# A fused retention and gated MLP kernel: another start, pair 3 transposed by DMA, and loads in turns behind a gate

## The chip, the cores and the metric

The kernel runs on one core of a Trainium2 chip. The metric is the device time in microseconds (us) of a whole execution, the median of several runs. A profile shows one execution: its span runs from the first to the last instruction of the core, and the execution's own time is somewhat longer.

## The reference

Linear attention with a decay per head (a retention layer), and behind it an MLP whose activation is h·cos(h):

```python
gamma = 1.0 - 2.0 ** (-5.0 - np.arange(H))
for t in range(S):
    state = gamma * state + einsum('bhd,bhe->bhde', k[:, :, t], v[:, :, t])
    y[:, :, t] = scale * einsum('bhd,bhde->bhe', q[:, :, t], state)
x = y.transpose(0, 2, 1, 3).reshape(B * S, H * D)
h = x @ w_in
out = (h * np.cos(h)) @ w_out
```

There are B = 4 batches, H = 8 heads, S = 768 positions and D = 64; x has 3072 rows of 512, w_in is 512 x 2048, w_out 2048 x 512. All inputs and the output are float32; inside, the products run in bf16.

## The kernel before

**Tiling.** A sequence is cut into 6 chunks of 128 positions. The unit of the attention is a *pair*: one chunk of two batches, so there are 12 pairs, numbered 0 to 11. Two pairs make a *group* of 512 rows for the MLP; there are 6 groups. A pair's q, k and v are float32 buffers of 128 positions x 8 heads x 64, one per batch (the two *halves* of a pair, 256 KB each). There are five sets of them, and `SLOT` says which set a pair uses.

**What a pair goes through.** `load` fetches q, k and v. `conv_q` multiplies q by its decay and `conv_v` does so with v, mostly on GpSimd; `conv_k` casts k to bf16 on ScalarE. Then q and k are transposed: either by `stage_t` (16 transposes on TensorE and two VectorE copies out of PSUM) or by `stage_t_dma` (two DMA transposes issued by SP, one for each half). `stage_a` (A) multiplies k by q, `stage_m` (M) applies the causal mask on VectorE, `half_y` (Y) forms the outputs of a half, with the carried state if the chunk isn't the first, and ScalarE copies them to `xt`, the MLP's input. `stage_s` (S) adds the chunk to the state in PSUM, and `state_out` copies that to `stb` for the next pair.

**What a group goes through.** `unit_f` is one of 16 units of the first MLP matmul: four matmuls over 512 rows, a sine on ScalarE (cos(h) = sin(h + pi/2)), and a product on VectorE into `gt`. `pair_f` is the same for the 256 rows of one pair, two units at a time, and `first_f` the first four units of group 0. `unit_o` is a quarter of a 128-row output tile: four matmuls; behind the fourth quarter ScalarE copies the tile to one of four buffers `ob`, and SP issues its copy to memory. In the main loop the units F of group g and O of group g-1 alternate, in 16 slots s per group.

**What sets the order.** The schedule is manual: each engine runs its instructions in the order in which the program text issues them, and waits by semaphores for data and for buffers. `Clock` and `Banks` are bookkeeping while the program is built: they choose which of the seven PSUM banks a unit takes, by an estimate of when each comes free. A bank is free once its reader on ScalarE or VectorE is done, so work that stands late in ScalarE's order holds TensorE's banks.

**The queues.** Loads are issued by GpSimd for the most part (L132, and L138 for k of pair 1, both halves in one transfer). SP issues the first q, the first k and the second q (L163), and q and a part of v of pairs 4 and 5 (L495 and L498). The DMA transposes (L240) and the output copies (L387) are SP's. GpSimd's loads of a pair stand behind the products of an earlier pair in its order. No load waits for a transpose unless a buffer makes it.

**Start.** Pairs 0 and 1 run ahead of everything, with dummy matmuls (`warm`) between their stages. In L465 to L475 the order is A(1, half 0), Y(0, half 0), A(1, half 1), S(0), Y(0, half 1), three dummies, Y(1, half 0), Y(1, half 1), S(1), and then `first_f` (L476).

**Later pairs.** Pairs 2 and 3 are transposed on TensorE (L485 and L505), pairs 4 to 11 by DMA. From pair 6 on the main loop decides by the slot (L588 to L603): at slots 0 and 8 `ahead(p + 1)` issues the products and casts of the next pair, a slot later its transposes, and further slots A, M, Y and, inside `later`, the next loads. The k casts of pairs 7, 8, 9, 10 and 11 so stand behind F units (2,0), (2,8), (3,0), (3,8) and (4,0), where (g, s) is slot s of group g.

Of the kernel before, what the change touches and what calls it, by code (L numbers as in the profile page):

```python
# [47 lines left out]
def kernel(  # L48
# [50 lines left out]

    qf = [[sb([128, H, D], FP32, f"qf{i}_{b}") for b in range(2)] for i in range(PRE)]  # L100
    kf2 = [sb([128, 2, H, D], FP32, f"kf{i}") for i in range(PRE)]
    kf = [[t[:, b] for b in range(2)] for t in kf2]
    vf = [[sb([128, H, D], FP32, f"vf{i}_{b}") for b in range(2)] for i in range(PRE)]
    ob = [sb([128, DM], FP32, f"ob{i}") for i in range(4)]
# [14 lines left out]
    gk = sb([128, NC, H], FP32, "gk")  # L119
    rel = sb([128, 128], FP32, "rel")  # L120


# [12 lines left out]

    def load_k(p):
        bp, c = divmod(p, NC)
        nc.gpsimd.dma_start(  # L138
            out=kf2[SLOT[p]].rearrange("p b h d -> p (b h) d"),
            in_=k[2 * bp : 2 * bp + 2, :, ds(c * C, C)].rearrange("b h t d -> t (b h) d"))  # L140

# [16 lines left out]
    def w_in_t(i, f):  # L158
# [3 lines left out]

    load(nc.sync, 0, ("q0", "k0", "q1"))  # L163
    nc.gpsimd.iota(pos, pattern=[[C, NC]], base=1, channel_multiplier=1,
                   allow_small_or_imprecise_dtypes=True)
    nc.gpsimd.iota(rel, pattern=[[1, 128]], base=0, channel_multiplier=-1,
                   allow_small_or_imprecise_dtypes=True)
    load(nc.gpsimd, 0, ("k1",))
    load(nc.gpsimd, 1, ("q0", "q1"))
    load_k(1)  # L170
    load(nc.gpsimd, 0, ("v0", "v1"))
# [292 lines left out]
    clk.run("pe", 0.0, 11.8)  # L464
    stage_m(1, stage_a(1, 0))  # L465
    half_y(0, 0)
    clk.run("pe", 0.0, 12.4)
    stage_m(1, stage_a(1, 1))
    stage_s(0, nc.scalar.copy)
    half_y(0, 1)  # L470
    warm(3)
    half_y(1, 0)
    banks.give(spare, clk.pe)
    half_y(1, 1)
# [7 lines left out]
    for u in range(12):  # L482
        unit_o(0, u % 4, u // 4)
        if u == 7:
            stage_t(2, 0)  # L485
            stage_t(2, 1)
            conv_v(2, nc.vector, (0,))
        elif u == 9:
            stage_m(2, stage_a(2, 0))
            conv_v(2, nc.vector, (1,))  # L490
        elif u == 11:
            stage_m(2, stage_a(2, 1))
    conv_k(3, True)
    conv_q(3, nc.gpsimd)
    load(nc.sync, 4, ("q0", "q1"))  # L495
    load(nc.gpsimd, 4, ("k0", "k1", "v0", "v1"))
    conv_v(3, nc.gpsimd)
    load(nc.sync, 5, ("q0", "q1", "v0"))  # L498
    load(nc.gpsimd, 5, ("k0", "k1", "v1"))
    for j in range(4):  # L500
# [3 lines left out]
    pair_f(2, 0)  # L504
    stage_t(3, 0)  # L505
    stage_t(3, 1)
    pair_f(2, 1)
    attend(3)
    conv_q(4, nc.gpsimd)
    conv_v(4, nc.gpsimd)  # L510
    conv_k(4, True)
    stage_t_dma(4)
    load(nc.gpsimd, 6, ("q0", "k0", "q1", "k1", "v0", "v1"))
    pair_f(2, 2)
    pair_f(2, 3, (0,))
    stage_y(3, nc.scalar.copy)
    pair_f(2, 3, (1,))
    conv_q(5, nc.gpsimd)
    conv_v(5, nc.gpsimd)
    load(nc.gpsimd, 7, ("q0", "k0", "q1", "k1", "v0", "v1"))  # L520
    pair_f(3, 0)
    conv_k(5, True)
    stage_t_dma(5)
    pair_f(3, 1)
    pair_f(3, 2)
    conv_q(6, nc.gpsimd)
    conv_k(6, True)
    conv_v(6, nc.gpsimd)
    pair_f(3, 3)

    def ahead(p):
        if p < NP:
            conv_q(p, nc.gpsimd)
            conv_k(p, True)
            conv_v(p, nc.gpsimd)

    def fetch(p):
        load(nc.gpsimd, p, ("q0", "k0", "q1", "k1", "v0", "v1"))

    def later(p):  # L540
        stage_y(p)
        n = 8 if p == 4 else p + 3 if p > 5 else NP
        if n < NP:
            fetch(n)

# [19 lines left out]
    attend(4)  # L565
    stage_t_dma(6)
    o_units(1, 2, 6)
    later(4)
    attend(5)
    o_units(1, 6, 10)  # L570
    later(5)

    for g in range(2, NG + 1):
        for s in range(16):
            hf, r = divmod(s, 8)
            p = 2 * (g + 1) + hf
# [9 lines left out]
            while late and late[0][0] <= 16 * g + s:  # L586
                late.pop(0)[1]()
            if p < NP:  # L588
                if r == 0:
                    ahead(p + 1)  # L590
                elif r == 1:
                    if p + 1 < NP:
                        stage_t_dma(p + 1)
                elif r == 2 and p in (6, 7, 8):
                    todo = [stage_a(p, b) for b in range(2)]
                    stage_m(p, todo[0])
                    put_off(16 * g + s + 1, lambda todo=todo, p=p: stage_m(p, todo[1]))
                elif r == 6 and p in (6, 7, 11):
                    later(p)
                elif (g, s) == (3, 4):  # L600
                    fetch(11)
                if (g, s) in joined:
                    join(joined[g, s], 16 * g + s)  # L603

# [29 lines left out]
```

## Time and profile before

| | us |
|---|---|
| median of 8 runs | 209.2 |
| lowest, highest | 209.01, 209.64 |
| the profiled execution's own time | 209.49 |
| its span | 207.7 |

| engine | busy us | share of the span |
|---|---|---|
| TensorE matmul (PE) | 200.2 | 96% |
| TensorE weight load (PEld) | 113.0 | 54% |
| VectorE (DVE) | 113.2 | 55% |
| ScalarE (ACT) | 114.4 | 55% |
| GpSimd (POOL) | 102.4 | 49% |

A busy time is the sum of an engine's instructions. GpSimd's includes the issuing of its loads here, though not that of other engines' DMAs, and its work ends at about 123 us of the span. TensorE is busy in nearly all of the span, and its granted clock is full throughout. The 16 DMA engines are close to fully busy from the start up to about 115 us and have little to do after that. In all, 27.26 MB are read from memory and 6.29 MB written. The chain of waits is followed back from the last instruction, at each step to what released it; a list of waits says which engine stood still, for whom, for how long in total, how often, and for how long at most. In a timeline a row has the start, the duration, the engine and line, the operation, and in brackets the idle time before it and what ended that.

### The profile page before, as it was taken

The numbers are of one execution on the slowest core, as the hardware profiler recorded it, in microseconds if no ns is written. First come the engines' busy times: TensorE is split into PE (matmuls) and PEld (weight loads), VectorE is DVE, ScalarE is ACT, GpSimd is POOL, SyncE is SP. The second block draws the span as 40 slices with busy tenths as digits, with TensorE's granted clock in tenths as the row PEclk, the third lists the DMA queues.
The fourth block names the chain that finished last, engine by engine and source line by source line (L and its number), as shares of the span: only waits on it lengthen the run. The fifth ranks groups of instructions, "written<-read, shape, count | busy, mean of one in ns | idle before, by whom it ended". The sixth has DMA issues, their size and how long they took to land.

```text
span 207.7 us, 4176 instructions
## 1 busy us (share of the span) xinstructions
PE 200.2 (96%) x1646; PEld 113.0 (54%) x1646; DVE 113.2 (54%) x188; ACT 114.4 (55%) x193; POOL 102.4 (49%) x118
## 2 busy tenths in 40 slices
PE   7689999999999999999999999999999999999993
PEld 2257554559897555546544465544465444444452
DVE  4691984554956563869874367853367244443000
ACT  6678873247997336577753754653554653553120
POOL 8999238399999999999996130000000000000000
PEclk9999999999999999999999999999999999999999
DMA  6999999999999999949999711161101101110212
GB/s 159 345 237 206 214 253 286 336 270 347 236 152 298 337 204 299 288 155 194 196 292 139 205 43 50 54 104 50 50 3 50 50 15 39 50 52 20 81 75 80
DMA packets 36644, 33.83 MB, mean 163 GB/s; under 512 B 26768, under 2 KB 29072, under 8 KB 36624
## 3 DMA queue, kind: packets, MB, share of 16 engines
q0 software_dynamic: 7808, 20.98, 39.1%
q1 hardware_dynamic: 28672, 12.49, 27.1%
q8 instruction: 13, 0.21, 0.4%
q10 hardware_dynamic: 144, 0.10, 0.1%
q14 instruction: 7, 0.06, 0.1%
HBM read 27.26 MB, written 6.29 MB: 162 GB/s over the span
## 4 chain that ended last, share of the span: by engine, by line
PE 92%; DMA 3%; DVE 2%; issue 1%; SPq 0%; ACT 0%; DVEq 0%
PE bank L379 39%; PE bank L338 32%; PE bank L349 7%; PE bank L257 3%; DMA qf<-in_q_dram 3%; PE bank L279 3%; PE bank L284 3%; PE bank L396 2%; PE st_ps L301 1%; DVE am L266 1%; PE bank L360 1%; PE bank L230 1%; PE bank L367 1%; DVE qkt L214 1%; SPq L132 0%
## 5 line engine op out<-in xcount | busy, mean ns | idle before, releaser
L331 DVE TENSOR_TENSOR gt<-bank,cosb 128x512 bf16<-128x512 f32 x96 | 64.9, 689 | 62.7 <-ACT cosb L327 62.5
L327 ACT ACTIVATE cosb<-bank,halfpi 128x512 bf16<-128x512 f32 x96 | 65.1, 688 | 49.9 <-PE bank L338 45.4
L379 PE MATMUL bank<-w_out_sb,gt 128*128 128x512 bf16 x368 | 89.6, 379 | 0.0
L338 PE MATMUL bank<-xt,w_in 128*128 128x512 bf16 x304 | 75.3, 380 | 0.0
L379 PEld LDWEIGHTS <-gt 128*128 128x128 bf16 x368 | 35.5, 98 | 41.3
L338 PEld LDWEIGHTS <-w_in 128*128 128x128 bf16 x304 | 33.9, 114 | 30.7
L266 DVE TENSOR_TENSOR am<-bank,mask 128x512 bf16<-128x512 f32 x48 | 30.4, 682 | 3.8 <-PE bank L257 3.7
L202 POOL TENSOR_TENSOR vs<-vf,gk 128x512 bf16<-128x512 f32 x21 | 21.4, 1044 | 6.0 <-PE st_ps L301 5.9
L386 ACT COPY ob<-bank 128x512 f32<-128x512 f32 x23 | 13.4, 587 | 17.9 <-PE bank L379 17.9
L132 POOL DMA_DIRECT2D vf<-in_v_dram x23 | 20.3, 885 | 4.6 <-DMA w_out_sb<-in_moe_w_out_dram 4.6
L195 POOL TENSOR_TENSOR qk<-qf,gq 128x512 bf16<-128x512 f32 x18 | 18.6, 1055 | 5.0 <-DMA qf<-in_q_dram 2.8
L132 POOL DMA_DIRECT2D kf<-in_k_dram x21 | 18.9, 901 | 1.8 <-DMA w_out_sb<-in_moe_w_out_dram 1.6
L208 ACT CAST qk<-kf 128x512 bf16<-128x512 f32 x24 | 14.0, 615 | 9.5 <-DMA kf<-in_k_dram 9.5
L288 ACT CAST xt<-bank 128x512 bf16<-128x512 f32 x24 | 13.0, 588 | 7.9 <-PE bank L284 7.8
L132 POOL DMA_DIRECT2D qf<-in_q_dram x18 | 16.2, 902 | 0.8 <-DMA w_in<-in_moe_w_in_dram 0.8
L349 PE MATMUL bank<-xt,w_in 128*128 128x256 bf16 x128 | 14.7, 273 | 0.0
L349 PEld LDWEIGHTS <-w_in 128*128 128x128 bf16 x128 | 13.8, 114 | 0.4
L284 PE MATMUL bank<-am,vs 128*64 128x128 bf16 x192 | 11.7, 220 | 0.0
L279 PEld LDWEIGHTS <-stb 128*64 128x64 bf16 x160 | 8.8, 109 | 4.3 <-issue 3.1
L279 PE MATMUL bank<-qkt,stb 128*64 128x128 bf16 x160 | 10.7, 222 | 0.1
L284 PEld LDWEIGHTS <-vs 128*64 128x64 bf16 x192 | 10.0, 110 | 0.5 <-issue 0.4
L313 DVE CAST stb<-st_ps 64x512 bf16<-64x512 f32 x12 | 8.2, 685 | 2.3 <-PE st_ps L301 2.1
(46 smaller groups left out, 85.5 us busy)
## 6 DMA issues: line engine op xcount, KB each, us to landing
vf<-in_v_dram POOLq DMA_DIRECT2D x23, 256.0 KB, 6.9
out_dram<-ob SPq DMA_DIRECT2D x23, 256.0 KB, 2.0
kf<-in_k_dram POOLq DMA_DIRECT2D x21, 256.0 KB, 6.7
qf<-in_q_dram POOLq DMA_DIRECT2D x18, 256.0 KB, 6.2
w_out_sb<-in_moe_w_out_dram POOLq DMA_DIRECT2D x4, 512.0 KB, 12.3
qf<-in_q_dram SPq DMA_DIRECT2D x6, 256.0 KB, 8.2
w_in<-in_moe_w_in_dram POOLq DMA_DIRECT2D x3, 512.0 KB, 8.1
kf<-in_k_dram POOLq DMA_DIRECT2D x1, 512.0 KB, 6.0
```

The source lines that it names most:

```text
L132: eng.dma_start(out=t[SLOT[p]][b], in_=src[2 * bp + b, :, ds(c * C, C)].rearrange("h t d -> t h d"))
L195: eng.tensor_tensor(out=qk[p % NB][:, b, 0], in0=qf[SLOT[p]][b], in1=bc(gq, p % NC), op=ALU.mult)
L202: eng.tensor_tensor(out=vs[p % NB][:, b], in0=vf[SLOT[p]][b], in1=bc(gk, p % NC), op=ALU.mult)
L208: nc.scalar.copy(out=qk[p % NB][:, b, 1], in_=kf[SLOT[p]][b])
L266: nc.vector.tensor_tensor(out=am[p % 2][b][j], in0=ap[j], in1=mask.unsqueeze(1).to_broadcast([128, HP, 128]), op=ALU.mult)
L279: nc.tensor.matmul(yp[ts(j, 64), a, :], lhsT=stb[p % 2][:, b, a, ts(j, 64)], rhs=qt(n, b, a), start=True, stop=False, skip_group_check=True)
L284: nc.tensor.matmul(yp[ts(j, 64), a, :], lhsT=vs[n][:, b, 2 * a + j, :], rhs=am[p % 2][b][j][:, a, :], start=(c == 0), stop=True, skip_grou ...
L327: nc.scalar.activation(out=cb, in_=bank, func=AF.Sin, bias=halfpi)
L331: nc.vector.tensor_tensor(out=out, in0=bank, in1=cb, op=ALU.mult)
L338: nc.tensor.matmul(bank, lhsT=w_in_t(i, f), rhs=xt[g % 2][:, i, :], start=(i == 0), stop=(i == KIN - 1))
L349: nc.tensor.matmul(bank[:, ts(e, 256)], lhsT=w_in_t(i, f + e), rhs=xt[g % 2][:, i, ts(hf, 256)], start=(i == 0 and e == 0), stop=(i == KIN ...
L379: nc.tensor.matmul(bank, lhsT=gt[g % 2][:, f, ts(j, 128)], rhs=w_out_sb[:, f, :], start=(f == 0), stop=(f == KOUT - 1))
```

## The change

- **First loads.** k of pair 0, half 0, is issued by ScalarE (its own hardware queue), q of pair 0, half 0, by SP, and after it q of pair 1, half 0. The second q of pair 0 is issued by GpSimd, behind the second k.
- **Order of the start.** S(0) comes directly behind A(1, half 0), then A(1, half 1), and then both halves of Y(0). The three dummies are split: one ahead of Y(1, half 0), two behind it.
- **Pair 3** is transposed by DMA, no longer on TensorE. Its k casts are issued at u = 9 of the loop over the first output units, no longer behind that loop.
- **Turns.** From pair 3 on, `turn(p)` issues on GpSimd the q products, has SP issue the DMA transposes, issues the v products, and then a copy of two columns out of the transposed k of half 0 into a scratch tile `gate`, which nobody reads. The loads of pair p+1 follow it, as three transfers of 512 KB (k, q, v, both halves in each). GpSimd works in order, so these loads aren't issued until the transposition of half 0 is complete. SP issues no loads any more after the start. The q, k and v buffers of a pair's two halves are now one tile.
- **Places.** The k casts get places of their own: pair 4 behind `pair_f(2, 0)`, pair 5 where it was, pair 6 within the first output units of group 1, and pairs 7 to 11 behind (2,0), (2,6), (2,12), (3,4) and (3,12). A and Y keep their places on TensorE.

```diff
-    qf = [[sb([128, H, D], FP32, f"qf{i}_{b}") for b in range(2)] for i in range(PRE)]
-    kf2 = [sb([128, 2, H, D], FP32, f"kf{i}") for i in range(PRE)]
-    kf = [[t[:, b] for b in range(2)] for t in kf2]
-    vf = [[sb([128, H, D], FP32, f"vf{i}_{b}") for b in range(2)] for i in range(PRE)]
+    both = {n: [sb([128, 2, H, D], FP32, f"{n}f{i}") for i in range(PRE)] for n in "qkv"}
+    qf, kf, vf = [[[t[:, b] for b in range(2)] for t in both[n]] for n in "qkv"]
...
+    gate = sb([128, 2], BF16, "gate")
...
-    def load_k(p):
+    def load_both(p, names):
         bp, c = divmod(p, NC)
-        nc.gpsimd.dma_start(
-            out=kf2[SLOT[p]].rearrange("p b h d -> p (b h) d"),
-            in_=k[2 * bp : 2 * bp + 2, :, ds(c * C, C)].rearrange("b h t d -> t (b h) d"))
+        for n in names:
+            nc.gpsimd.dma_start(
+                out=both[n][SLOT[p]].rearrange("p b h d -> p (b h) d"),
+                in_=SRC[n][1][2 * bp : 2 * bp + 2, :, ds(c * C, C)].rearrange(
+                    "b h t d -> t (b h) d"))
...
-    load(nc.sync, 0, ("q0", "k0", "q1"))
+    load(nc.scalar, 0, ("k0",))
+    load(nc.sync, 0, ("q0",))
+    load(nc.sync, 1, ("q0",))
...
-    load(nc.gpsimd, 0, ("k1",))
-    load(nc.gpsimd, 1, ("q0", "q1"))
-    load_k(1)
+    load(nc.gpsimd, 0, ("k1", "q1"))
+    load(nc.gpsimd, 1, ("q1",))
+    load_both(1, "k")
...
     stage_m(1, stage_a(1, 0))
+    stage_s(0, nc.scalar.copy)
+    clk.run("pe", 0.0, 13.0)
+    stage_m(1, stage_a(1, 1))
     half_y(0, 0)
-    clk.run("pe", 0.0, 12.4)
-    stage_m(1, stage_a(1, 1))
-    stage_s(0, nc.scalar.copy)
     half_y(0, 1)
-    warm(3)
+    warm(1)
     half_y(1, 0)
+    warm(2)
...
             conv_v(2, nc.vector, (1,))
+            conv_k(3, True)
         elif u == 11:
             stage_m(2, stage_a(2, 1))
-    conv_k(3, True)
-    conv_q(3, nc.gpsimd)
-    load(nc.sync, 4, ("q0", "q1"))
-    load(nc.gpsimd, 4, ("k0", "k1", "v0", "v1"))
-    conv_v(3, nc.gpsimd)
-    load(nc.sync, 5, ("q0", "q1", "v0"))
-    load(nc.gpsimd, 5, ("k0", "k1", "v1"))
+    def turn(p):
+        conv_q(p, nc.gpsimd)
+        stage_t_dma(p)
+        conv_v(p, nc.gpsimd)
+        if p + 1 < NP:
+            nc.gpsimd.tensor_copy(out=gate, in_=qkt[p % NB][:, 0, 1, HP - 1, 126:])
+            load_both(p + 1, "kqv")
+
+    turn(3)
...
     pair_f(2, 0)
-    stage_t(3, 0)
-    stage_t(3, 1)
+    conv_k(4, True)
     pair_f(2, 1)
     attend(3)
-    conv_q(4, nc.gpsimd)
-    conv_v(4, nc.gpsimd)
-    conv_k(4, True)
-    stage_t_dma(4)
-    load(nc.gpsimd, 6, ("q0", "k0", "q1", "k1", "v0", "v1"))
+    turn(4)
...
     attend(4)
-    stage_t_dma(6)
-    o_units(1, 2, 6)
-    later(4)
+    o_units(1, 2, 4)
+    conv_k(6, True)
+    o_units(1, 4, 6)
+    turn(6)
+    stage_y(4)
...
+    k_at = {(2, 0): 7, (2, 6): 8, (2, 12): 9, (3, 4): 10, (3, 12): 11}
+    t_at = {(2, 1): 7, (2, 8): 8, (2, 15): 9, (3, 6): 10, (3, 13): 11}
+    a_at = {(2, 2): 6, (2, 10): 7, (3, 2): 8}
+    y_at = {(2, 6): 6, (2, 14): 7, (4, 14): 11}
...
-            if p < NP:
-                if r == 0:
-                    ahead(p + 1)
-                elif r == 1:
-                    if p + 1 < NP:
-                        stage_t_dma(p + 1)
...
+            at = (g, s)
+            if at in k_at:
+                conv_k(k_at[at], True)
+            if at in t_at:
+                turn(t_at[at])
```

More of the change, by code (lines that the diff above doesn't have):

```diff
@@ L517 @@
     pair_f(2, 3, (1,))
-    conv_q(5, nc.gpsimd)
-    conv_v(5, nc.gpsimd)
-    load(nc.gpsimd, 7, ("q0", "k0", "q1", "k1", "v0", "v1"))
     pair_f(3, 0)
     conv_k(5, True)
-    stage_t_dma(5)
     pair_f(3, 1)
+    turn(5)
     pair_f(3, 2)
-    conv_q(6, nc.gpsimd)
-    conv_k(6, True)
-    conv_v(6, nc.gpsimd)
     pair_f(3, 3)
-    def ahead(p):
-        if p < NP:
[L533 to L544, printed above, removed]
     late = []
@@ L565 @@
     attend(4)
-    stage_t_dma(6)
-    o_units(1, 2, 6)
-    later(4)
+    o_units(1, 2, 4)
[3 more added lines that the diff above has]
+    stage_y(4)
     attend(5)
     o_units(1, 6, 10)
-    later(5)
+    stage_y(5)
+    k_at = {(2, 0): 7, (2, 6): 8, (2, 12): 9, (3, 4): 10, (3, 12): 11}
+    t_at = {(2, 1): 7, (2, 8): 8, (2, 15): 9, (3, 6): 10, (3, 13): 11}
+    a_at = {(2, 2): 6, (2, 10): 7, (3, 2): 8}
+    y_at = {(2, 6): 6, (2, 14): 7, (4, 14): 11}
     for g in range(2, NG + 1):
         for s in range(16):
-            hf, r = divmod(s, 8)
-            p = 2 * (g + 1) + hf
             if g == 2 and s % 2 == 0 and s < 12:
@@ L585 @@
                     last_o(g - 1, 3)
-            while late and late[0][0] <= 16 * g + s:
+            now = 16 * g + s
+            while late and late[0][0] <= now:
                 late.pop(0)[1]()
-            if p < NP:
-                if r == 0:
-                    ahead(p + 1)
-                elif r == 1:
-                    if p + 1 < NP:
-                        stage_t_dma(p + 1)
[L594 to L603, printed above, removed]
+            at = (g, s)
[3 more added lines that the diff above has]
+                turn(t_at[at])
+            if at in a_at:
+                p = a_at[at]
+                todo = [stage_a(p, b) for b in range(2)]
+                stage_m(p, todo[0])
+                put_off(now + 1, lambda todo=todo, p=p: stage_m(p, todo[1]))
+            if at in y_at:
+                stage_y(y_at[at])
+            if at in joined:
+                join(joined[at], now)
 _INS = ['q', 'k', 'v', 'moe_w_in', 'moe_w_out']
```

## The prediction

> **What bounds the kernel now.** First the shares along the chain of waits, then the list of TensorE's waits, then the chain in order of time.
>
> ```profile
> PE 92%; DMA 3%; DVE 2%; issue 1%; SPq 0%; ACT 0%; DVEq 0%
> ```
>
> ```profile
> PE bank L413 <- DVE gt L172: 1.2, 1, 1.2
> PE bank L257 <- DVE qkt L214: 1.1, 2, 0.6
> PE bank L230 <- DVE qk L195: 1.1, 1, 1.1
> PE bank L230 <- ACT qk L208: 0.4, 1, 0.4
> ```
>
> ```profile
> 1.88 5.99 DMA qf<-in_q_dram
> 7.93 0.57 issue
> 8.51 1.28 DVE am L266 x2
> ...
> 49.55 0.89 PE bank L230 x16
> ...
> 98.89 1.85 PE bank L338 x8
> ```
>
> TensorE sets the end, and all its waits (3.8 us in four rows) lie in the first 13 us; behind that, matmul follows matmul to 204 us. So time can be won only by removing TensorE work or shortening the head, and lost wherever TensorE is made to wait. The head hangs on the second q of pair 0 (issued 1.88, landed 7.87), then on a full VectorE. The row at 49.55 is the 16 transposes of pair 3. The row at 98.89 is two units of four matmuls; its second half (99.8) is the first unit of group 3 and reads what ScalarE copied for pair 7.
>
> The cover of that copy is seen in ScalarE's timeline:
>
> ```profile
> 98.25 1.06 ACT L288 CAST xt<-bank 128x512 bf16<-128x512 f32 x2
> 99.92 0.69 ACT L327 ACTIVATE cosb<-bank,halfpi 128x512 bf16<-128x512 f32 x1 [0.60 <-PE bank L338]
> 100.78 0.69 ACT L327 ACTIVATE cosb<-bank,halfpi 128x512 bf16<-128x512 f32 x1 [0.18 <-PE bank L338]
> 101.37 1.13 ACT L208 CAST qk<-kf 128x512 bf16<-128x512 f32 x2
> ```
>
> The copies end at 99.3, half a us ahead of TensorE. The two k casts of pair 9 (101.37) stand behind them, where no one is in a hurry.
>
> For the price of DMA I read GpSimd's timeline, windows (the last three columns: TensorE's clock, DMA share, GB/s) and a transpose's time to landing:
>
> ```profile
> 92.11 0.93 POOL L132 DMA_DIRECT2D qf<-in_q_dram  x1
> ```
>
> ```profile
> 51.00:54.00 3.00, 3.00 (x39) 2.70 (x38) 2.90 (x6) 2.46 (x5) 3.00 (x4) 1.00 1.05 367
> 92.25:93.25 1.00, 1.00 (x6) 0.46 (x4) 0.11 (x1) 1.00 (x3) 1.00 (x2) 1.00 0.00 0
> 93.25:94.75 1.50, 1.50 (x22) 0.91 (x21) 1.09 (x2) 1.06 (x2) 1.50 (x2) 1.00 0.86 203
> ```
>
> ```profile
> qkt<-qk SPq DMA_TRANSPOSE x1, 3.4
> ```
>
> A load that GpSimd issues into idle engines (92.11) moves no byte for about 1.3 us; in a stretch mostly of loads 367 GB/s flow; a DMA transpose with no load beside it (issue 116.54) lands after 3.4 us, and its partner, issued 1.3 us later, after 2.9. Beside loads transposes took 4.6 to 12.9 us.
>
> **What the Trainium skill says.** "DMA: Bandwidth & Descriptors", section "Issuing engines are not separate DMA queues": transfers of all issuers run on the same 16 engines, and another issuer saves only issue time. The head agrees: three loads issued by 1.88 us landed at 3.6, 5.0 and 7.9, with GpSimd's between. The same page, "Anatomy of one DMA", gives a fixed part of about 2 us per GpSimd transfer besides its bytes. Here 1.3 us are seen ahead of the first byte; behind the last I take 0.4 (SP's output copy of 256 KB at 139.62 lands after 2.0 us with its bytes between 140.25 and 141.5).
>
> **The change part by part.**
>
> *Head.* The same bytes are asked for. k of pair 0 goes out at about 0.74 on ScalarE instead of 1.26; it delays ScalarE's table load by some 0.5 us, covered by the casts, which wait for data until 5.01. The second q becomes GpSimd's second load; that place landed at about 7.7 before (issue 2.44, 5.3 us), with shared engines starting earlier perhaps 7.4, against 7.87. VectorE behind it is full: 8 us to the last mask product. So I take 0.45 us. S ahead of Y moves the state casts on ScalarE from 14.32 to about 13.3 and keeps Y(1) from waiting for them; the mask products still end last, so it only makes the 0.45 pass through to the first F. Bounds: 0 (GpSimd's second load no sooner) to 0.8.
>
> *Pair 3.* Its 16 transposes leave TensorE: 0.89 us, full gain, for nothing waits around 49.55; two VectorE copies (1.36 us) go as well. Its DMA transposes replace them. q of pair 3 lands at 39.8 and 41.5 before; SP's loads of pair 4, 0.5 MB then in flight, are gone, so 1 us sooner. First transpose issued at 40.1, last landed by about 46; TensorE needs them at about 51.7. Hidden by 5 us. Sum of the gains: 0.45 + 0.9 = 1.35, say 1.4 us.
>
> *The turns.* GpSimd now does, for pair p: two q products, two v products, a two-column copy that waits for p's first transposition, and then three loads of 512 KB for p+1 (before: products and loads without that wait, 9.3 us a pair). The copy holds back everything behind it on GpSimd, so each pair's data are a serial chain: q product of one half 1.05; SP's reaction 0.05; transpose 3.4; the copy 0.2 (estimate from 128x6 iota, 0.15; 0.1 to 0.3); first byte 1.3; k and q, 1.05 MB at 367 GB/s, 2.85; completion 0.4. Sum 9.25. The v products (to 4.1 us) lie beside the transpose. Output copies add: 256 KB is 0.7 us, one per turn, somewhat over half in the way: 0.45. Turn 9.7 us; bounds 9.25 (no collision) and 10.1 (transposes 3.7, 340 GB/s, output in full).
>
> *Where the chain starts.* Pair 3's first transposition lands at about 44.5, beside the tail of v; the copy passes at 44.7. k4 lands at 48.6 (3.2 alone, plus one output copy), q4 at 50.5 (four output copies are under way from 43). Product and transpose of pair 4: issued 51.6, landed 55.1, passed 55.4. k5 lands at 58.6. Then one turn each: k6 68.3, k7 78.0, k8 87.7, k9 97.4.
>
> *Where they are needed.* Transposes have slack (pair 6: about 76 against 80.1; others 4 us and more). The k casts don't: they stand in ScalarE's order, and each wait holds the sines, output copies and xt copies behind it. On the schedule shortened by 1.4, ScalarE comes to k5 at 59, k6 68.3, k7 78.3, k8 86.8, k9 95.2. k8 and k9 have been moved ahead, to 8.4 us apart, less than a turn. k5 to k7 cost nothing. k8 late by 0.9: behind it stand xt copies, three sines and an output copy, of which TensorE needs the last at about 92.7 (unit 11); it costs 0 to 0.3, contained in what follows. k9: behind the two casts (1.13) are two sines (1.3) and both xt copies of pair 7 (1.06), 3.5 us, and TensorE can't begin group 3 (98.4 on this schedule) without them. So k9 must land by 94.9; at 97.4 TensorE waits 2.5 us. k10 is asked for 12.7 us later and k11 later still: the debt is paid once. With both ends of start and turn, k9 lands between 95 and 99.7, so the wait is 0.1 to 4.8; I take 2.5.
>
> *Rest.* Loads of 512 KB instead of 256 KB save GpSimd issues (three of 1.15 for six of 0.88); GpSimd was busy until 115 and sets no end, so nothing. SP's order moves each transposition ahead of an output copy; four output buffers cover that.
>
> Sum: 209.49 - 1.4 + 2.5 = 210.6 against the profiled execution. It lies 0.3 above the median of 209.2, so 210.3.
>
> **The rivals.** *The turns fit.* If a turn takes 9.3 us or less, or pair 4 starts a us sooner, k9 lands before 95.9, the wait in front of group 3 shrinks under 1 us, and the gains win: at best 207.8. For it: the sum without output copies is 9.25, and the casts' places (59, 68.3, 78.3) are about that far apart. Against: k9 stands only 8.4 behind k8, and each turn has six handovers, of which I price the small ones low. The deciding point is k9 against 95.9. *Turns aren't strict.* The copy reads the first half's transposition only, so the second is still under way when loads start, as are output copies; where such things met before (93 to 101) transposes took 7 to 10 us. A turn of 10.5 makes k9 land at about 100.5: wait 5.6, 213.4. For it: DMA was saturated at 9.3 us per pair before. Against: a second transposition lands 0.9 us after the first, ahead of a load's first byte.
>
> **How the numbers follow.** Wait for k9: 0.50, 209.6 to 212.3. About balanced (wait 1.0 to 1.8): 0.12, 208.8 to 209.6. Turns fit: 0.28, 207.5 to 208.8. Turns much longer: 0.10, about 213.4. What this kernel's measurement can tell from no change is 0.2% (0.4 us). Faster is the third case, 0.28; same the second, 0.12; slower the others, 0.60. The likeliest gives 210.3, own range 209.6 to 212.3; the range over the cases is 207.6 to 212.8.
>
> **What would show it.** Right: an idle stretch of 2 to 3 us on TensorE near 98 to 101, with an xt copy as releaser; ScalarE idle before the k casts (L211 of the new text) on a DMA of kf, longest for pair 9; GpSimd's two-column copies 9.5 to 10 us apart; the transposes near 49.5 gone; the first F about 0.4 us sooner. Wrong: no TensorE wait behind 20 us (then about 207.8), waits of the A products (L260) for DMA transposes instead of for xt, or a head that isn't shorter.

## The result and the profile after

| | us |
|---|---|
| before, median of 32 runs (lowest to highest) | 209.35 (208.72 to 212.02) |
| after, median of 11 runs (lowest to highest) | 231.51 (227.29 to 232.41) |
| after, the profiled execution; its span | 226.88; 224.8 |
| ratio after to before, 95% interval | 1.094, 1.0911 to 1.097 |

The change makes the kernel about 9% slower, where 0.5% was forecast. The ratio leaves six disturbed executions out, which is why it lies below the quotient of the medians; the five others took 227.29 to 230.66 us, 229.0 in the mean, and experiments are set against these. The profiled execution is quicker than all eleven. The sum below is reckoned on its span: 224.8 against 207.7, so 17.1 us have to be found.

From the page: busy time of TensorE with the count of its instructions, its clock in 40 slices (in tenths of full speed, 9 is full), and the chain that ended last, by engine.

```profile
PE 207.8 (92%) x1630; PEld 114.7 (51%) x1630; DVE 111.9 (50%) x186; ACT 114.3 (51%) x193; POOL 94.2 (42%) x107
...
PEclk9999999999999979599958999999999999999999
...
PE 48%; DMA 28%; POOL 15%; issue 4%; ACT 2%; DVE 0%; POOLq 0%; ACTq 0%; DVEq 0%
```

The chain was 92% TensorE; now over half of it is DMA, GpSimd and others. And two things are new that no count of waits shows: the clock falls in three places, and with it TensorE's busy time *grows* from 200.2 to 207.8 us, though it has fewer matmuls.

TensorE's waits (engine, line, what it waited for: us in total, times, longest):

```profile
PE bank L341 <- ACT xt L291: 4.2, 1, 4.2
PE bank L341 <- ACT ob L389: 3.2, 1, 3.2
PE bank L382 <- ACT xt L291: 2.5, 1, 2.5
...
PE bank L352 <- DVE gt L334: 0.6, 1, 0.6
```

Behind 20 us they add up to 10.9 us, where there were none. All three large ones end with a copy by ScalarE. What ScalarE itself waited for, in its own list:

```profile
ACT qk L211 <- DMA kf<-in_k_dram: 24.9, 12, 5.6
```

L211 is the k cast. In ScalarE's timeline the copies that TensorE missed are seen right behind three such casts:

```profile
75.58 1.14 ACT L211 CAST qk<-kf 128x512 bf16<-128x512 f32 x2 [5.60 <-DMA kf<-in_k_dram]
76.63 1.06 ACT L291 CAST xt<-bank 128x512 bf16<-128x512 f32 x2
...
87.65 1.14 ACT L211 CAST qk<-kf 128x512 bf16<-128x512 f32 x2 [3.33 <-DMA kf<-in_k_dram]
88.70 0.68 ACT L330 ACTIVATE cosb<-bank,halfpi 128x512 bf16<-128x512 f32 x1
89.28 0.57 ACT L389 COPY ob<-bank 128x512 f32<-128x512 f32 x1
...
111.47 1.14 ACT L211 CAST qk<-kf 128x512 bf16<-128x512 f32 x2 [4.15 <-DMA kf<-in_k_dram]
112.51 1.26 ACT L330 ACTIVATE cosb<-bank,halfpi 128x512 bf16<-128x512 f32 x2
113.66 1.07 ACT L291 CAST xt<-bank 128x512 bf16<-128x512 f32 x2
```

These are the casts of pairs 6, 7 and 9. TensorE resumes at 77.26, as the first of the two copies in the row at 76.63 ends, at 89.90, as the copy of `ob` at 89.28 ends, and at 114.78, as the row at 113.66 ends. Why k is late is read from GpSimd's timeline, one whole turn:

```profile
77.13 2.04 POOL L198 TENSOR_TENSOR qk<-qf,gq 128x512 bf16<-128x512 f32 x2 [4.61 <-DMA qf<-in_q_dram]
79.13 2.04 POOL L205 TENSOR_TENSOR vs<-vf,gk 128x512 bf16<-128x512 f32 x2
81.12 0.18 POOL L503 COPY gate<-qkt 128x2 bf16<-128x2 bf16 x1
81.63 1.19 POOL L138 DMA_DIRECT2D kf<-in_k_dram  x1 [0.33 <-issue]
82.82 1.15 POOL L138 DMA_DIRECT2D qf<-in_q_dram  x1
83.96 1.16 POOL L138 DMA_DIRECT2D vf<-in_v_dram  x1
89.39 2.04 POOL L198 TENSOR_TENSOR qk<-qf,gq 128x512 bf16<-128x512 f32 x2 [4.27 <-DMA qf<-in_q_dram]
```

From 77.13 to 89.39 a turn takes 12.3 us. The gate copies stand at 44.49, 57.23, 68.47, 81.12, 93.39, 105.00, 117.03 and 129.95, so the mean turn is 12.2. The gate itself has nothing to wait for, but for 1.1 us before the last: it comes 4.0 us after the q products began, and the transposes have landed by then (2.8 us in the median). From the gate to the next q product pass 8.3 us here, and 8.0 in the mean of seven turns. GpSimd is idle for half of that.

The clock is read from windows (start and end; width; busy us and count of PE, PEld, DVE, ACT and POOL; granted clock; DMA share; GB/s):

```profile
87.00:88.00 1.00, 0.00 (x0) 0.00 (x0) 0.00 (x0) 0.35 (x1) 0.00 (x0) 1.00 0.97 324
88.00:89.00 1.00, 0.00 (x0) 0.00 (x0) 0.00 (x0) 1.00 (x3) 0.00 (x0) 0.91 0.97 328
89.00:90.00 1.00, 0.10 (x1) 0.10 (x1) 0.59 (x1) 1.00 (x3) 0.61 (x1) 0.50 0.43 143
90.00:92.00 2.00, 2.00 (x6) 0.62 (x6) 1.63 (x4) 0.64 (x2) 2.00 (x3) 0.50 0.21 51
92.00:94.00 2.00, 2.00 (x6) 0.72 (x5) 1.84 (x4) 0.49 (x1) 1.67 (x4) 0.50 0.96 216
94.00:96.00 2.00, 2.00 (x7) 0.74 (x6) 0.47 (x2) 0.69 (x1) 2.00 (x2) 0.59 0.57 153
```

TensorE stands from 86.7 to 89.9. At 88.8 its clock drops to half, and it stays there for 6.8 us, until 95.6, long after matmuls run again; four matmuls take 1.86 us in place of 1.03. In the same way the clock is at half from 78.6 to 82.0 (3.4 us, behind the wait of 2.5 us that ended at 77.26) and from 112.7 to 119.5 (6.8 us). The Trainium skill, "TensorE: Matmul & The Clock Gate", Part 1, section "HAM oscillation — how this bites in real kernels", has the rule "no PE-idle gaps >~3.4µs". The trace agrees in kind, but not in the length: a wait of 2.5 us was enough here, and in two experiments waits of 3.3 and 3.5 us passed at full clock (see e7). The three stretches, 17.1 us at half speed, are 8.5 us of full speed, the same as (1 - 0.962) x 224.8 from the mean clock.

The sum: 10.9 of waits + 8.5 of lost clock - 1.1 of gains (0.2 in the head, 0.9 of transposes) = 18.3, against 17.1 found. About 3 us of the low clock fall on time in which TensorE stood anyway (88.8 to 89.9 and 112.7 to 114.8), which takes 1.6 off the sum: 16.7.

### The profile page after: what moved, and what is told of

Read it like the earlier page. It is cut to its first block, busy times and chain, and to the rows that moved or that the text cites. A ratio compares the mean times of both kernels' runs of the same rounds, so it can differ in the third digit from the quotient of the medians.

```text
span 224.8 us, 4106 instructions
## 1 busy us (share of the span) xinstructions
PE 207.8 (92%) x1630; PEld 114.7 (51%) x1630; DVE 111.9 (50%) x186; ACT 114.3 (51%) x193; POOL 94.2 (42%) x107
## 4 chain that ended last, share of the span: by engine, by line
PE 48%; DMA 28%; POOL 15%; issue 4%; ACT 2%; DVE 0%; POOLq 0%; ACTq 0%; DVEq 0%
PE bank L382 23%; PE bank L341 19%; DMA qf<-in_q_dram 14%; DMA kf<-in_k_dram 8%; DMA w_out_sb<-in_moe_w_out_dram 6%; POOL vs L205 6%; POOL qk L198 3%; POOL kf L138 2%; PE bank L399 2%; POOL kf L131 1%; POOL qf L131 1%; PE bank L282 1%; PE bank L260 1%; ACT qk L211 1%; PE bank L352 1%
## 5 line engine op out<-in xcount | busy, mean ns | idle before, releaser
L382 PE MATMUL bank<-w_out_sb,gt 128*128 128x512 bf16 x368 | 92.3, 387 | 2.5 <-ACT xt L291 2.5
L341 PE MATMUL bank<-xt,w_in 128*128 128x512 bf16 x304 | 79.0, 393 | 7.4 <-ACT xt L291 4.2
L341 PEld LDWEIGHTS <-w_in 128*128 128x128 bf16 x304 | 34.5, 116 | 41.0 <-issue 12.0
L211 ACT CAST qk<-kf 128x512 bf16<-128x512 f32 x24 | 13.9, 616 | 24.9 <-DMA kf<-in_k_dram 24.9
L352 PEld LDWEIGHTS <-w_in 128*128 128x128 bf16 x128 | 13.8, 114 | 1.1 <-issue 0.7
L287 PE MATMUL bank<-am,vs 128*64 128x128 bf16 x192 | 12.5, 228 | 0.4 <-DVE am L269 0.4
L138 POOL DMA_DIRECT2D kf<-in_k_dram x9 | 10.7, 1189 | 2.3 <-issue 1.8
L282 PE MATMUL bank<-qkt,stb 128*64 128x128 bf16 x160 | 11.5, 232 | 0.0
L287 PEld LDWEIGHTS <-vs 128*64 128x64 bf16 x192 | 10.5, 115 | 0.5 <-issue 0.4
L416 PE MATMUL bank<-gt 128*128 128x512 bf16 x22 | 8.4, 495 | 1.2 <-DVE gt L175 1.2
L260 PE MATMUL bank<-qkt 64*128 64x128 bf16 x192 | 8.2, 218 | 1.3 <-DVE qkt L217 1.1
L138 POOL DMA_DIRECT2D qf<-in_q_dram x8 | 9.2, 1152 | 0.0
## 6 DMA issues: line engine op xcount, KB each, us to landing
w_out_sb<-in_moe_w_out_dram POOLq DMA_DIRECT2D x4, 512.0 KB, 12.2
```

Of the source, the lines that this page charges most:

```text
L138: nc.gpsimd.dma_start(out=both[n][SLOT[p]].rearrange("p b h d -> p (b h) d"), in_=SRC[n][1][2 * bp : 2 * bp + 2, :, ds(c * C, C)].rearrang ...
L211: nc.scalar.copy(out=qk[p % NB][:, b, 1], in_=kf[SLOT[p]][b])
L282: nc.tensor.matmul(yp[ts(j, 64), a, :], lhsT=stb[p % 2][:, b, a, ts(j, 64)], rhs=qt(n, b, a), start=True, stop=False, skip_group_check=True)
L287: nc.tensor.matmul(yp[ts(j, 64), a, :], lhsT=vs[n][:, b, 2 * a + j, :], rhs=am[p % 2][b][j][:, a, :], start=(c == 0), stop=True, skip_grou ...
L341: nc.tensor.matmul(bank, lhsT=w_in_t(i, f), rhs=xt[g % 2][:, i, :], start=(i == 0), stop=(i == KIN - 1))
L352: nc.tensor.matmul(bank[:, ts(e, 256)], lhsT=w_in_t(i, f + e), rhs=xt[g % 2][:, i, ts(hf, 256)], start=(i == 0 and e == 0), stop=(i == KIN ...
```

## The experiments

**The theory** after the result: a turn with only one pair's loads in flight takes 12 us, ScalarE's order asks for k more often than that, the k casts hold the copies behind them, and each wait costs more than its length, because the clock falls. **Rivals**: the gate copy is what slows the turn; contention in the DMA engines makes the loads slow, with or without turns; the places of the casts, not the turn, are at fault; the clock has another cause than idle time.

One table serves all of them: in each profile, the waits of TensorE behind 20 us and the clock lost ((1 - mean clock) x span) against what the span is above that of before (207.7). Kernels made from after have its 1.1 us of gains to be taken off; e5 has 0.5, e6 1.4, e7 none.

| kernel | median us (runs) | profiled us | waits | clock lost | span above before |
|---|---|---|---|---|---|
| after | 231.51 (11) | 226.88 | 10.9 | 8.5 | 17.1 |
| e1 two pairs ahead | 215.21 (4) | 214.96 | 4.8 | 1.9 | 5.5 |
| e2 late casts | 220.78 (2) | 223.04 | 11.0 | 3.3 | 13.6 |
| e3 no gate | 223.26 (2) | 222.41 | 11.4 | 3.5 | 12.9 |
| e4 halves | 219.45 (2) | 221.24 | 10.0 | 1.8 | 11.3 |
| e5 head alone | 208.92 (22) | 209.00 | 0 | 0 | -0.5 |
| e6 head and pair 3, no turns | 240.75 (6) | 240.25 | 24.5 | 13.6 | 30.8 |
| e7 before with three waits | 226.98 (4) | 226.58 | 11.7 | 5.4 | 17.0 |
| e11 two ahead, halves | 214.33 (4) | 215.33 | 6.7 | 0.2 | 5.9 |
| e12 the same, late casts | 212.78 (4) | 213.42 | 3.4 | 1.7 | 4.0 |
| e14 q first | 226.6 (2) | 225.25 | 13.6 | 5.4 | 15.8 |

Waits and lost clock less the gains give the last column within 1.2 us in every row but e14 (2.1 too much) and e6 (6 too much); there the low clock inside a wait, which is counted twice, is the larger part of the difference.

**e1: the loads two pairs ahead.** The gate and the order stay; only the pair that is loaded behind a gate is another.

```diff
-            load_both(p + 1, "kqv")
+            for n in (4, 5) if p == 3 else (p + 2,):
+                if n < NP:
+                    load_both(n, "kqv")
```

> Theory D (depth): the loads are late because each pair's loads start only when the pair before has gone through its products, so that only one pair is ever under way. With the loads two pairs ahead, gate and transposes kept: no wait of ScalarE for k beyond 1 us, no TensorE wait behind 20 us, clock at full; 208.0 to 208.8 us. Rival C (capacity): loads and transposes together fill the DMA engines for 12 us a pair, whatever the order. Then k of pairs 7 to 9 lands hardly sooner, and it stays above 220 us.

Measured: 215.21 us, ratio to before 1.0253 (1.0181 to 1.0326). So the one pair in flight makes up most of the loss, some 14 of 20 us, but not all of it. GpSimd's and TensorE's waits in this kernel:

```profile
POOL gate L503 <- DMA qkt<-qk: 23.9, 7, 4.4
```

```profile
PE bank L260 <- DMA qkt<-qk: 3.1, 3, 2.4
```

Now the gate is where GpSimd stands, and TensorE waits for transposes at the A products (L260): with a second set of loads in flight the transposes land after 5.7 us in the median instead of 2.8. The waits for k shrank from 24.9 to 10.5 us. The turns themselves are hardly shorter: from 61.88 to 130.02 the gates stand 11.4 us apart in the mean. What changes is that k lands a turn earlier, ahead of its cast. My expectation missed this residue.

**e2: three casts later.** The casts of pairs 8, 9, 10 and 11 stand one to three slots later in ScalarE's order.

```diff
-    k_at = {(2, 0): 7, (2, 6): 8, (2, 12): 9, (3, 4): 10, (3, 12): 11}
+    k_at = {(2, 0): 7, (2, 7): 8, (2, 15): 9, (3, 6): 10, (3, 13): 11}
```

> The k casts of pairs 8 to 11 stand 1 to 3 slots later, just ahead of their transposes; loads as in the changed kernel. Theory D: the 12 us of a turn stay, so k and q of pairs 6 to 8 are as late as before, but less work stands behind the waiting casts: two of the three long waits shrink, about 214 to 220 us. If the casts' places alone were the fault: 208 to 210. If the places don't matter: 226 to 231.

Measured: 220.78 us (218.52, and 223.04, which is the profiled one). The wait in front of group 3 is gone from the list, and a wait of 5.0 us for `ob` stands elsewhere; the turn is still 12 us and more (12.5 in the mean). The places matter by some us; they don't cure it.

**e3: no gate.** The copy of two columns is left out, so the loads follow the v products directly. No output depends on the copy.

```diff
-            nc.gpsimd.tensor_copy(out=gate, in_=qkt[p % NB][:, 0, 1, HP - 1, 126:])
```

> Leaves out the two-column copy that waits for the transposition. Theory D: the copy waited for a transposition only once (1.1 us), GpSimd's v products end at the same time; a turn gets shorter by the copy and its issue, 0.5 us, so pair 9 comes about 3 us sooner; 218 to 226 us. Rival G (the gate is the brake): without it loads overlap transposes as in the kernel before, turn 9.5 us, 208 to 211.

Measured: 223.26 us, ratio 1.0679 (1.0618 to 1.074); the q products stand 10.9 to 12.4 us apart, 11.7 in the mean against 12.0 in after. The turn is nearly as long without the gate: GpSimd's order alone, q product, v product, loads of the next pair, makes it. The rival "the gate is the brake" falls, though leaving it out gains some 5 us (1.068 against 1.094).

**e4: the turn's loads in halves.** Six transfers of 256 KB instead of three of 512 KB.

```diff
-            load_both(p + 1, "kqv")
+            load(nc.gpsimd, p + 1, ("k0", "q0", "k1", "q1", "v0", "v1"))
```

> The loads of a turn in six transfers of 256 KB, in the order k, q, k, q, v, v. If the large transfers are what lands late: turn 10.5 us or less, under 218 us. If the serial chain is: the same landing time or 0.5 us worse through the longer issue on GpSimd, 226 to 233 us.

Measured: 219.45 us (217.65, and 221.24, which is the profiled one). Between the first turn (13.7 us) and the last (12.7) they take 10.3 to 11.2 us, between the two expectations; the mean of all is 11.3. The first q product needs only half of k and q, and starts while the rest is under way.

**e5: the head alone.** The kernel before with the change's first loads and order of the start, and nothing else.

```diff
-    load(nc.sync, 0, ("q0", "k0", "q1"))
+    load(nc.scalar, 0, ("k0",))
+    load(nc.sync, 0, ("q0",))
+    load(nc.sync, 1, ("q0",))
...
-    load(nc.gpsimd, 0, ("k1",))
-    load(nc.gpsimd, 1, ("q0", "q1"))
+    load(nc.gpsimd, 0, ("k1", "q1"))
+    load(nc.gpsimd, 1, ("q1",))
...
+    stage_s(0, nc.scalar.copy)
+    clk.run("pe", 0.0, 13.0)
+    stage_m(1, stage_a(1, 1))
     half_y(0, 0)
-    clk.run("pe", 0.0, 12.4)
-    stage_m(1, stage_a(1, 1))
-    stage_s(0, nc.scalar.copy)
...
```

> The kernel before with the change's first loads and start order alone. The changed kernel's first F began 0.2 us sooner than before, not 0.45: 0.1 to 0.3 us faster, about 209.0 us (0.999). If the start were worth what was forecast: 0.45 us.

Measured: 208.92 us against 209.20, ratio 0.9986 (0.9975 to 0.9997): 0.3 us, small, but the interval leaves 1 out. In its profile the first F begins at 16.33 (before: 16.82). This is the one version that beat both kernels.

**e6: the head and pair 3 by DMA, without turns.** e5 with pair 3's transposition moved from TensorE to SP, the loads as before.

```diff
     conv_q(3, nc.gpsimd)
+    stage_t_dma(3)
...
-    stage_t(3, 0)
-    stage_t(3, 1)
```

> The same with pair 3 transposed by DMA, loads as in the kernel before. 16 transposes of TensorE fewer: a further 0.9 us, together 1.1 us, 208.1 us (0.995), if the DMA transposes, which now meet the loads of pairs 4 and 5, land by 51 us. If they are slowed to 9 us or more as beside loads elsewhere: TensorE waits 1 to 3 us and it is no faster than before.

Measured: one run of 217.37 us and five of 239.16 to 245.54; the profile is of one of these, 240.25. TensorE's waits and SP's timeline in it:

```profile
PE bank L259 <- DMA qkt<-qk: 24.5, 6, 8.4
```

```profile
40.81 2.76 SPq L242 DMA_TRANSPOSE qkt<-qk  x2
43.66 7.48 SPq L132 DMA_DIRECT2D qf<-in_q_dram  x4
...
57.86 40.47 SPq L242 DMA_TRANSPOSE qkt<-qk  x6
```

Pair 3's own transposes are in time (issued from 40.81, landed after 2.9 and 4.3 us). But SP's loads of pairs 4 and 5 now stand behind them in its queue, and the issue of the next six transposes stretches over 40 us (20 in e5); to landing a transpose takes 12.3 us in the median, a load about 10. I expected 208.1 and was wrong: even the quick run is 8.5 us above e5. Whether the transposes and loads in each other's way are to blame, or that SP's loads of pairs 4 and 5 start 8.6 us later than in e5 (43.66 against 35.07), and why the time scatters over 28 us, this run doesn't settle. So it doesn't show either what the turns are good for.

**e7: what a wait costs.** Before, with three added waits late in the kernel where nothing else is tight: GpSimd copies a piece of `gt` and works for a set time, and one added matmul (3 x 0.39 us in all) reads the result.

```diff
+    def stall(g, f, n):
+        nc.gpsimd.tensor_copy(out=dly, in_=gt[g % 2][:, f, :])
+        for i in range(n):
+            nc.gpsimd.tensor_tensor(out=dly.rearrange("p (h d) -> p h d", h=H),
+                                    in0=qf[0][0], in1=bc(gq, 0), op=ALU.mult)
+
+    def meet():
+        bank = banks.take()
+        nc.tensor.matmul(bank, lhsT=dly[:, :128], rhs=dly, start=True, stop=True,
+                         skip_group_check=True)
...
+    holds = {(4, 4): 4, (5, 1): 5, (5, 10): 7}
```

> The kernel before with three added waits of TensorE, made by a chain on GpSimd: about 2, 3 and 5 us long, at three places of the last groups. The clock's price measured by itself. Theory K: a wait[...] drops the granted clock to 0.5 for 3 to 7 us behind it, so that this wait costs its length and 2 to 3.5 us more; the 2 us wait costs its length alone. Total 10 + 2 to 7 us. If waits cost their length alone: 10 us and a clock of 1.0.

Measured: 226.98 us, ratio 1.0844 (1.0793 to 1.0895). The three waits in TensorE's timeline (in brackets their length):

```profile
146.43 0.39 PE L563 MATMUL bank<-dly 128*128 128x512 bf16 x1 [2.35 <-POOL dly L558]
...
175.89 0.39 PE L563 MATMUL bank<-dly 128*128 128x512 bf16 x1 [3.54 <-POOL dly L558]
...
199.32 0.61 PE L563 MATMUL bank<-dly 128*128 128x512 bf16 x1 [5.81 <-POOL dly L558]
```

and the clock behind each, from windows with columns as above:

```profile
147.00:149.00 2.00, 2.00 (x11) 0.96 (x9) 0.56 (x1) 1.10 (x2) 0.00 (x0) 1.00 0.00 0
...
177.00:179.00 2.00, 2.00 (x6) 0.71 (x5) 0.64 (x1) 0.69 (x1) 0.00 (x0) 0.50 0.00 0
...
196.00:198.00 2.00, 0.00 (x0) 0.00 (x0) 0.00 (x0) 0.00 (x0) 1.92 (x2) 0.76 0.00 0
...
200.00:202.00 2.00, 2.00 (x6) 0.75 (x5) 0.00 (x0) 0.32 (x1) 0.00 (x0) 0.50 0.00 0
```

The wait of 2.35 us left the clock whole; the one of 3.54 us halved it for 3.4 us (176.5 to 180.0), beginning when matmuls already ran again; the one of 5.81 us halved it for 6.8 us (197.0 to 203.8), of which 4.5 lie behind the wait. 11.7 us of waits and 1.2 us of added matmuls cost 17 us of span. Next to no DMA moves in these windows, and what else was added, GpSimd's work, stands ahead of the first wait too, where the clock stayed. So it is TensorE's idle time that brings the clock down; the rival of another cause is out.

The length of a wait alone doesn't decide, though. e3 has two long waits and one drop (its waits of TensorE, and its clock in 40 slices):

```profile
PE bank L341 <- ACT ob L389: 6.2, 1, 6.2
PE bank L341 <- ACT xt L291: 3.3, 1, 3.3
...
PEclk9999999999999999599999999999999999999999
```

The wait of 6.2 us that ended at 89.40 took the clock down; the one of 3.3 us that ended at 112.93 left it whole, and so did one of 3.5 us in e14, while one of 2.4 us was enough in e1. What decides can be read from the traces. Within a profile the drops lie whole multiples of 3.41 us apart: those of after, at 78.58, 88.82 and 112.72, 3 and 7 times. So each trace can be cut into stretches of 3.41 us that end at such points. Behind 20 us, and the idle end of a kernel aside, all profiles together have 27 drops. In 26 of them TensorE had stood still for 2.05 us or more of the stretch before (1.93 in the other); in stretches without a drop it stood for 2.02 at most. The clock came back after stretches with at most 0.8 us of idle time. The 3.33 us in e3 fall on two stretches, 1.66 on each; the 2.35 us of e7 are 1.74 and 0.61; of the 2.52 us in after, 2.09 lie in one. No run here moved a wait across such a point on purpose, so this is a regularity of the traces, not one that was put to a test.

**e8 and e9: a turn's loads with next to nothing beside them.** e9 is after with a further set of loads of 512 KB and one of 256 KB, issued in group 5, where DMA has little to do; nobody uses what they bring.

```diff
+            if at == (5, 3):
+                nc.gpsimd.tensor_copy(out=dly, in_=gt[1][:, 3, :2])
+                load_both(7, "kqv")
+            if at == (5, 10):
+                nc.gpsimd.tensor_copy(out=dly, in_=gt[1][:, 10, :2])
+                load(nc.gpsimd, 8, ("k0", "q0", "k1", "q1", "v0", "v1"))
```

e8 lacks the two copies, so that GpSimd had nothing to wait for and issued both sets directly behind pair 11's loads; it says nothing on the question.

> The changed kernel with two extra sets of loads in a quiet stretch, into buffers that nobody reads any more: three of 512 KB in the order k, q, v, and later six of 256 KB. Measures landing without transposes or other loads. If the large loads' landing is their own: q lands 6 us or more after its issue as in a turn (6.3). If it is what shares the engines in a turn: 3.5 to 4.5 us.

> The changed kernel with the two extra sets of loads again, each now held back by a copy on GpSimd until group 5, where DMA has nothing but an output copy now and then; nobody reads what they load. If the large loads' landing is their own: first load lands 5.5 us or more after its issue, q 6 us or more, as in a turn. If the tail of the transposes and the output copy delay them in a turn: first 3.5, second 4, third 4.5 us.

Measured in e9: k, q and v, issued at 191.81, 192.99 and 194.13, landed after 5.1, 6.2 and 7.7 us, so q 7.4 us after the first issue. In the turn shown above it was 7.7. k is a little sooner than the 5.5 us that I had set for it, q is not. The rival "contention makes a turn's loads slow" is out: they are nearly as slow alone.

**e10: TensorE kept busy.** After, with 44 dummy matmuls in front of the three large waits, 9.5 us of added work.

```diff
+    FILL = {5: 14, 6: 14}
...
+        if b == 0:
+            dummies(bk[0], FILL.get(p, 0))
...
+        dummies(bank, 16 if (g, f) == (3, 0) else 0)
```

> The changed kernel with 44 dummy matmuls more on TensorE (14 ahead of A of pair 5, 14 ahead of A of pair 6, 16 ahead of the first unit of group 3), 9.5 us of extra work inside its three long waits. Theory K (idle time halves the clock): the waits become short, the clock stays at 1.0, and it gets 5 to 9 us faster than the changed kernel, 220 to 225 us. If the lower clock is not for idleness: as slow as the changed kernel or slower by what the dummies push back, 228 to 240 us.

Measured: 226.84 us (226.28 to 227.42), clock lost 1.8 us in place of 8.5. With 9.5 us more to do it is no slower than after: its ratio to before is 1.082 (1.0795 to 1.0844), against 1.094, which is 2.5 us less, while of the profiled executions this one is 0.5 us longer. That speaks for the price of the clock, but less than I expected: dummies also push the A products and all behind them back, and waits of 2.5 and 2.0 us remain. How much of it is which, this run doesn't tell.

**e11 and e12: the best of the turns.** e11 puts e1 and e4 together. e12 is e11 with e2's places, and the cast of pair 4 behind `attend(3)`.

```diff
+            for n in (4, 5) if p == 3 else (p + 2,):
+                if n < NP:
+                    load(nc.gpsimd, n, ("k0", "q0", "k1", "q1", "v0", "v1"))
...
-    conv_k(4, True)
     pair_f(2, 1)
     attend(3)
+    conv_k(4, True)
```

> Loads two pairs ahead, in transfers of 256 KB. Depth took off 14 us and halves 10 us when each was alone. If both gains have the same source (data sooner), little more than depth alone: 211 to 215. If they add: 206 to 209, level with the kernel before.

> Loads two pairs ahead in 256 KB transfers, and in addition the k casts of pairs 4 and 8 to 11 just ahead of their transposes. If the remaining 5 us are waits behind casts (gt and xt, 3.3 us of 6.3 in the run before): 210 to 212. If they are the DMA transposes' lateness beside the loads: 213 to 216.

Measured: e11 214.33 us, ratio 1.0232 (1.0184 to 1.028); e12 212.78, ratio 1.0153 (1.0125 to 1.0181), between its two expectations. The gains of e1 and e4 don't add, since both mend the same thing. What e12 still waits for:

```profile
PE bank L260 <- DMA qkt<-qk: 3.4, 2, 3.0
```

No wait for `xt` or `ob` is left: the casts no longer hold TensorE. One late transposition does, and behind its 3.0 us the clock is at half for 3.4 us (75.0 to 78.4). 3.4 + 1.7 of clock - 1.1 is 4.0, which is the span's surplus to the tenth.

**e13: k and q alone.** What in the loading of a turn is long? When q lands in the turn at 81.63, some 1.5 MB of loads have moved (1.7 MB since 83.5, less an output copy of 0.26), nearly all of k, q and v. So v's bytes could be what holds q up. Here v is issued a turn later, behind the q products.

```diff
         conv_q(p, nc.gpsimd)
         stage_t_dma(p)
+        if p > 3:
+            load_both(p, "v")
         conv_v(p, nc.gpsimd)
...
-            load_both(p + 1, "kqv")
+            load_both(p + 1, "kq")
```

> In each turn only k and q of the next pair are issued behind the gate copy; v is issued in the next turn, behind its q products and DMA transposes. If v's bytes are what holds q up (1.57 MB shared instead of 1.05 MB, about 300 GB/s), the time from a gate copy to the next q product falls from 8.3 us to 6.4 to 6.9 us and the k load lands at about the same 5.3 us or up to 1 us sooner. If q's bytes are through and only its completion is late, the time stays at 7.8 to 8.4 us. The v products then wait for v, so a whole turn gets longer in both cases (13 to 15 us) and the kernel slower than 230 us.

Measured: 275.41 us (one run). From a gate copy to the next q product pass 7.7, 7.3, 7.4, 7.3, 7.1, 7.1 and 6.9 us, 7.3 in the mean against 8.0 in after: between the two expectations. Of the 0.7 us, 0.3 are a shorter step from the gate copy to the issue of k (0.12 here, 0.44 in after), so v's bytes cost about 0.4 us; most of the time stays with k and q alone. Windows of GpSimd with the clock, the DMA share and GB/s as the last three columns; k is issued at 107.05, q at 108.23, and the product begins at 114.27:

```profile
108.00:108.50 0.50, 0.50 (x2) 0.50 0.00 0
108.50:109.00 0.50, 0.50 (x1) 0.50 0.23 25
109.00:109.50 0.50, 0.38 (x1) 0.50 0.90 98
109.50:110.00 0.50, 0.00 (x0) 0.50 0.84 139
110.00:110.50 0.50, 0.00 (x0) 0.50 0.91 344
...
112.00:112.50 0.50, 0.00 (x0) 0.50 0.90 287
112.50:113.00 0.50, 0.00 (x0) 0.50 0.65 221
113.00:113.50 0.50, 0.00 (x0) 0.50 0.15 49
```

Here the 7.2 us lie open. 1.5 us to the first byte; 1.5 us more in which only 25 to 139 GB/s are moved, though for 1 us of it the engines are nearly fully busy; 3.1 us of flow at about 300 GB/s; and 1.1 us from the end of the flow to the product.

**e14: q first.** The order of the turn's loads is q, k, v.

```diff
-            load_both(p + 1, "kqv")
+            load_both(p + 1, "qkv")
```

> The turn's three loads go out as q, k, v instead of k, q, v. If the chain is set by q's landing alone, the q product starts about 1.5 us sooner and the turn falls from 12.2 to about 10.8 us; k lands 1.2 us later after its gate, but the gates come sooner, so k of pairs 6, 7 and 9 lands 1.5 to 4 us sooner than after: 218 to 223 us. If the k casts are the brake in the turn too (the DMA transposes need k cast by ScalarE), the turn stays at about 12 us and the time at 226 to 231.

Measured: 226.6 us (225.25 and 227.94), turns of 11.2 to 12.8 us, 12.0 in the mean: the figure of the second expectation, but not for its reason, the k casts. The q products come 2 us sooner after the gate, and the v products then wait for v, until the turn is as long as before. All three loads are in the chain, in whatever order.

## Why the prediction failed

**The direction and the mechanism were right.** The k casts wait in ScalarE's order, the `xt` copies of pair 7 behind the cast of pair 9 make TensorE wait at the start of group 3 (4.2 us), the gates make each pair's data a serial chain on GpSimd, and the transposes had slack. What failed are two terms of size, and one conclusion drawn from the first.

**The turn (9.7 us, bounds 9.25 to 10.1) is 12.2.** The failed term is the landing: first byte 1.3, k and q at 367 GB/s 2.85, completion 0.4, in all 4.55. e13 measures the same with nothing beside it: 1.5, then 4.6 for the bytes (1.5 us of it at a trickle), then 1.1, in all 7.2; the turn adds about 0.4 for v and 0.4 for the step from the gate to the issue. The first byte was nearly right. The flow was priced with a rate that was read from a stretch in which many loads were under way, and the completion with that of another queue's output copy. What the trickle comes from stays open. The Trainium skill's fit in "DMA: Bandwidth & Descriptors", section "Anatomy of one DMA", 2.0 us plus the bytes at 436 GB/s, would have erred the same way: worked out for 1.05 MB it gives an estimate of 4.4. The other terms of the turn were right or too high: the transposes took 2.8 and not 3.4 us, and didn't count, since the v products (to 4.1 us) reach further; the outputs' 0.45 can't be told apart.

**"k5 to k7 cost nothing", and k9's 2.5 us once.** This follows from the turn. The forecast had k6 at 68.3, k7 at 78.0 and k9 at 97.4. Their casts began at 75.6, 87.65 and 111.5. So three casts were late by enough to reach TensorE, not one, and the debt was paid three times: 2.5 + 3.2 + 4.2 us, where 2.5 was charged. That it was paid in front of group 3 for k9, as named, is the part that came out. k8, which was to come late, wasn't waited for: ScalarE, held back by the others, came to it only at 98.8.

**A wait was priced at its length.** That left out the clock. All three waits brought it down to half, for 3.4, 6.8 and 6.8 us; 8.5 us of full speed are missing. e7 shows the price by itself. This is the second large term.

**The gains.** Pair 3's transposes are off TensorE for good (0.9, as charged): its DMA transposes landed at about 44.3, far ahead of need. The head was charged with 0.45. In after the first F starts 0.18 us sooner, in e5 0.49, and e5's time is 0.3 us lower, so 0.2 to 0.5: within the bounds given.

**The rivals.** "Turns aren't strict" came nearest, with a longer turn and a time above the forecast. Its reason, the second transposition and the outputs beside the loads, was not the main cause, since e9 and e13 have nearly the same landing without them, and its 10.5 us were too low as well. Its evidence was real in another place: in e1, with a second set of loads in flight, the transposes took 5.7 us. The observations named in advance that came out: ScalarE idle ahead of L211 on kf, the copy of `xt` as the releaser, the transposes at 49.5 gone. That the gates would stand 9.5 to 10 us apart is the one that fell first.

## What to carry to other kernels

A chain with one load in flight pays each time for the whole of the load, from issue to landing, so price it by the landing time of the same size in the trace, not by bytes over a rate; a second set in flight took some 14 us off this kernel (ratio 1.094 to 1.025), and transfers in halves 8 to 11 (two runs). A wait of TensorE can cost more than its length: waits of 2.4 to 5.8 us put the clock at half for 3.4 or 6.8 us, so add up to half of that. Every wait over 3.6 us went with a low clock here; below that, down to 2.4, it hung on where the wait fell. And before work that waits on a DMA is moved on an in-order engine, look at what stands behind it there: the cast itself was in no hurry, the copies behind it were.

## What was not expected of the hardware

- Loads of 512 KB that GpSimd issued with no other transfer under way moved at a trickle for 1 to 1.5 us behind the first byte (25 to 139 GB/s at a DMA share of up to 0.9 in e13), so that full flow began about 3 us after the first issue: 3.0 in e13 (107.05 to 110.0), 3.2 in e9 (191.81 to 195.0), 2.9 in after (117.57 to 120.5).
- The clock can fall *behind* a wait, when matmuls already run again: in e7 at 176.5, the wait of 3.54 us having ended at 175.89; in after at 78.6, 1.3 us behind a wait of 2.52. From the start of the waits to the drop it was 2.1 to 4.2 us in after, e7 and e12, and the low clock lasted 3.4 or 6.8 us, in e6 and e13 also 10.2 and 13.7: always a multiple of 3.41. A wait of 2.35 us passed without it, and so did the 3.33 us in e3 and 3.52 us in e14, which fell on two stretches (see e7).
